# Attention beside four Strassen-style products on one NeuronCore: GpSimd ordered behind VectorE on their shared port, traced durations in the planner, a shorter hold for scores

## Chip, core and metric

One NeuronCore of one Trainium2 chip runs the whole program. The metric is device time in microseconds (us), the median over executions. Before the change it is 2990.05 us (2988.33 to 2990.17 in 3 runs).

## What is computed

Two independent blocks, joined along the last axis, all in fp32 with S = 2048, D = 1024, 32 heads of 32:

```python
qkv = x @ wqkv                                  # A: attention
p = softmax(q @ k.T * 32**-0.5); o = p @ v      # per head
a = concat(o) @ wo
re = xb @ dft_hid_re.T; im = xb @ dft_hid_im.T  # B: Fourier mixing
b = dft_seq_re @ re - dft_seq_im @ im
out = concat([a, b], axis=-1)
```

## The kernel before

**Dense work.** The four dense products (qkv, the two of block B, the output projection) are each cut into 2 by 2 blocks and done with seven products instead of eight, which needs sums and differences of blocks of both operands. Each operand tile of 128x512 is then split into a high half (a cast to the fast matmul format, L477, on VectorE or in some stages ScalarE) and a low half (tile minus high half, L480, on GpSimd or VectorE), and every product is three matmuls: high*high, low*high, high*low (L391, tiles `slot`, `h`, `l`). The sums of blocks are `fetch`'s tensor_tensors (L455, GpSimd or VectorE). PSUM results leave through VectorE (L629, L681, L896, L907).

**Attention.** For each head and each half row of scores a pair of matmuls (a "score pair", L1198) fills a PSUM tile `psS` of 128x1024. There are two such buffers. VectorE reads it once, writing the negated scores to `srow` and their minimum to `negm` (L1206, called the move below); ScalarE takes the exponentials and their sums from `srow` (L1212). The row maxima go back through DRAM into `qs`, and then the scores are computed a second time, transposed, 128x512 at a time (`psT`, L1328, two buffers), exponentiated by ScalarE (L1332, `pt` or `ptl`), and multiplied with V (L1347) in three runs per head whose results VectorE collects in `ot` (L1358, L1360). GpSimd or VectorE applies 1/sum (L1376).

**What sets the order.** Nothing is ordered by hand. While the program is recorded, a planner (`Plan`) plays it forward with a list of costs: at each moment of its own clock it starts, on each engine, the ready instruction of lowest rank, and that order is what each engine then runs, strictly in order. TensorE takes attention work (streams S, T, V: score pairs, transposed scores, V products) when it is ready and the dense "fills" otherwise. A score pair counts as ready `SLATE` us after its PSUM buffer is free by the plan, a transposed score `LATE` us after. The planner knows of one port that GpSimd and VectorE share: GpSimd instructions and those VectorE instructions marked `two=True` (casts, tensor_tensors from SBUF) are not started while `port` lies ahead of its clock (`choose`). That holds in the plan alone. On the chip an instruction waits for its data, for its buffer and for its engine's queue, and for nothing else.

Where the plan says that a GpSimd instruction comes after a cast, but the cast is late and the GpSimd instruction has its data, GpSimd goes first.

Of the kernel before, what the change touches and what calls it, by code (L numbers as in the profile page):

```python
# [10 lines left out]
AF = mybir.ActivationFunctionType  # L11
ALU = mybir.AluOpType
# [50 lines left out]
class Plan:  # L63
# [3 lines left out]

    LAT = 0.1
    LAT_PE = 0.2
    OVERLAP = {"ACT": 0.13, "DVE": 0.08, "POOL": 0.08}  # L70

    SLACK = {("SP", "POOL"): 2.0, ("SP", "DVE"): 2.0, ("SP", "PE"): 2.0, ("POOL", "DVE"): 0.7}
    KB_US = 360.0
    LANDING = 1.6
    QUEUE = 1.0

    def __init__(self):
        self.now = 0.0
        self.free = {e: 0.0 for e in ("PE", "ACT", "DVE", "POOL", "SP")}
        self.pending = {e: [] for e in ("ACT", "DVE", "POOL", "SP")}  # L80
        self.able = {e: [] for e in ("ACT", "DVE", "POOL", "SP")}
        self.dma = 0.0
        self.port = 0.0
        self.lane = [0.0] * 8
        self.seq = 0

    def op(self, engine, cost, emit, after=(), uses=(), rank=0.0, kb=0, order=None, other=None, lanes=1, two=False):

# [36 lines left out]

    def start(self, o, e=None):
        e = e or o.engine
        o.emit(e) if o.other else o.emit()
        o.begun = True
        self.free[e] = self.now + (o.cost if e == o.engine else o.other[1])  # L130
        if e == "POOL" or e == "DVE" and o.two:
            self.port = self.free[e]
        if o.kb:
            for _ in range(o.lanes):
                t = max(self.free[e], self.lane[0])
                self.dma = max(self.dma, t) + o.kb / o.lanes / self.KB_US
                o.end = self.dma + self.LANDING
                self.lane = self.lane[1:] + [o.end]
                if o.lanes > 1:
                    self.free[e] = t + o.cost  # L140
        else:
            o.end = self.free[e]
            self.free[e] -= self.OVERLAP.get(e, 0.0)
        for t in o.then:
            t.ready = max(t.ready, self.after(o, e, t))
            t.left -= 1
            if t.left == 0:
                self._release(t)
        for t in o.soon:
            t.ready = max(t.ready, self.now)  # L150
            t.left -= 1
            if t.left == 0:
                self._release(t)
        o.then = o.soon = ()
        o.emit = None
# [56 lines left out]
def kernel(  # L212
# [11 lines left out]
    nc = tc.nc  # L224
# [26 lines left out]
    def f(ap):  # L251
        return ap.bitcast(F32)
# [31 lines left out]
    rec = const.tile([P, 2 * NS], F32, name="rec")  # L284
# [50 lines left out]

    MM, PV, SWITCH, TINY = 0.2275, 0.853, 0.40, 0.17
    ES, ET = 1.235, 0.625
    MOVE = 1.25  # L340
    MAX, EVAC, CAST, BIT = 1.22, 0.685, 0.415, 0.275
    SUB = 1.31
    ISSUE = 0.46

    LATE, SLATE = 0.25, 1.2
    HB = 0
    ACAST = 0.6
    RES = 400
    SST = 13
    LEAD = 3.0  # L350
# [2 lines left out]
    NEAR = 0.2  # L353
# [3 lines left out]
    ATT = H * (128 * MM + 16 * PV + 3 * SWITCH)  # L357

    pl = Plan()
    op = pl.op  # L360
    att_on, t_on = [True], [False]
    nbank = [0]
# [54 lines left out]
    def fetch(shape, terms, store=None, keep=None):  # L417

        box = {}
        raws, seconds, tile_of, gate = where[0]  # L420
        rank = seq()
        sign, *first = terms[0]
        loaded = len(first) == 2
        if len(terms) == 1 and not loaded:
            return first[0].get, first[0].made, first[0].users
        if keep is None:
            old, users = raws.take()
        else:
# [12 lines left out]
        for sign, *term in terms[1:]:  # L441
            other = {}
            if len(term) == 2:
                gold, gusers = seconds.take()

                def load(src=term[0], other=other):
                    other["q"] = tile_of(shape, "g", len(seconds.users))
                    nc.sync.dma_start(other["q"], src)

                q = op("SP", ISSUE, load, gold + term[1] + gate, [gusers], rank, 256, seconds)  # L450
            else:
                other["k"], q, gusers = term[0], term[0].made, term[0].users

            def add(e, sign=sign, other=other, a=None if last is not None else first[0]):
                (nc.gpsimd if e == "POOL" else nc.vector).tensor_tensor(  # L455
                    out=dest(), in0=dest() if a is None else a.get(), in1=other["q"] if "q" in other else other["k"].get(), op=ALU.add if sign > 0 else ALU.subtract)

            last = op("POOL", SUB, add, old + [first[0].made if last is None else last, q], [users, gusers] + ([first[0].users] if last is None else []),
                      rank, 0, raws if keep is None and last is None else None, other=("DVE", ADD, 20 + rank), two=True)
            old = []  # L460
        if keep is not None:
            keep.made = last
        if store is not None:
            store[1].append(op("SP", ISSUE, lambda: nc.sync.dma_start(store[0], dest()), [last], [users], rank, 256))
        return dest, last, users
# [3 lines left out]
    def halves(raw, made, users, hi, lo, old, mine, order=(None, None)):  # L469

        rank = seq()

        def high(e=None):
            if e == "ACT":
                nc.scalar.activation(hi(), raw(), AF.Copy)
            else:
                nc.vector.tensor_copy(hi(), raw())  # L477

        def low(e):
            (nc.gpsimd if e == "POOL" else nc.vector).tensor_tensor(out=lo(), in0=raw(), in1=f(hi()), op=ALU.subtract)  # L480

        a = op("DVE", CAST, high, [made] + old[0], [users, mine[0]], 10 + rank, 0, order[0], ("ACT", ACAST, 25 + rank) if spare[0] else None, two=True)
        b = op("POOL", SUB, low, [a] + old[1], [users, mine[0], mine[1]], rank, 0, order[1], other=("DVE", ADD, 25 + rank), two=True)
        return a, b
# [687 lines left out]
    def scores(h):  # L1172
        ST = {}
# [11 lines left out]
        for n, (qt, c) in enumerate([(k % 4, k // 4) for k in range(8)] + [divmod(k, 2) for k in range(8, 32)]):  # L1185
            old, users = psS_r.take()
            own = h > 0 and qt < 4
            box = {}
# [29 lines left out]
            b = op("DVE", MOVE if h else MAX, mx, [a] + (sold if n == 0 else []) + (rold if h else []), [users, suse, *([ruse] if h else [])], 0)  # L1218
# [19 lines left out]
            nc.vector.tensor_reduce(out=box["l"][:, 0], in_=ST["negm"].rearrange("p c n -> p n c"), axis=AX.X, op=ALU.min)  # L1238

        def low():  # L1240
            nc.vector.tensor_tensor(out=box["l"][:, 1], in0=ST["nm"], in1=f(box["l"])[:, 0], op=ALU.subtract)

        b = op("DVE", TINY, high, maxes + lold, [luse, suse], -2)
        a = op("DVE", TINY, nmin, maxes + nold, [nuse, suse], -2)
# [14 lines left out]
    def sums(h):  # L1259
        ST, suse, nuse, exps, _ = mine[h]  # L1260
        box = {}
        told, tuse = small["tw"].take()

        def sub():
            box["t"] = sm.tile([P, 2, NS], F32, name="tt", bufs=1)
            for c in range(2):
                nc.vector.tensor_tensor(out=box["t"][:, c], in0=ST["nm"], in1=ST["negm"][:, c], op=ALU.subtract)

        def ex():
            nc.scalar.activation(box["t"], box["t"], AF.Exp)  # L1270

        def inv():
            w = box["t"]
            l = rec[:, 0:NS]
            nc.vector.tensor_tensor(out=w, in0=w, in1=ST["sums"], op=ALU.mult)
            nc.vector.tensor_reduce(out=l, in_=w.rearrange("p c n -> p n c"), axis=AX.X, op=ALU.add)
            nc.vector.reciprocal(l, l)
            box["l"] = sm.tile([P, 2 * NS], F32, name="ll", bufs=1)
            nc.vector.transpose(box["l"], rec)

        def spread():
            rt[h] = att_low().tile([P, NB], F32, name="rt", bufs=1)
            r = r_d[h][0:NS].rearrange("(j q) p -> j (q p)", j=4)
            for j in range(4):
                nc.sync.dma_start(rt[h][j * DH : j * DH + DH], r[j : j + 1].broadcast_to([DH, NB]))

        a = op("DVE", 0.24, sub, exps + told, [tuse, suse, nuse], -2, two=True)
        b = op("ACT", BIT, ex, [a], [tuse], -2)
        c = op("DVE", 0.84, inv, [b], [tuse, suse], -2, two=True)
        e = op("SP", ISSUE, lambda: nc.sync.dma_start(r_d[h].rearrange("q (g p) -> g q p", g=4), box["l"]), [c], [tuse], -2, 32)  # L1290
        rold, ruse = rt_r.take()
        g = op("SP", ISSUE, spread, [e, *rold], [ruse], -2, 256, lanes=4)
        rts[h] = (g, ruse)
# [224 lines left out]
```

## Time and profile before

| | |
|---|---|
| median of 3 runs | 2990.05 us (2988.33 to 2990.17) |
| profiled execution, device time | 2990.43 us |
| its span on the core | 2988.7 us |
| TensorE busy | 2957.1 us, 99% |
| VectorE busy | 2395.0 us, 80% |
| ScalarE busy | 2301.3 us, 77% |
| GpSimd busy | 930.1 us, 31% |
| granted TensorE clock, mean | 0.998 |

In the profile PE is TensorE's matmuls, PEld its weight loads, DVE VectorE, ACT ScalarE, POOL GpSimd, SP the queue that issues the DMAs. L and a number is a line of the kernel. A row of the timeline has the start, the duration, the engine, line and operation, the tiles, how many equal neighbours were merged, and in brackets the idle time before it with what ended it. Matmuls overlap, so that a busy TensorE can still be waiting: what counts is the distance between starts.

### The profile page before, as it was taken

To read this page: it belongs to the slowest core of one execution; us is meant where nothing else is said; L and a number is where in the kernel's file an instruction comes from. 1 tells how busy PE (TensorE), PEld (TensorE's weight loads), DVE (VectorE), ACT (ScalarE), POOL (GpSimd) and SP (SyncE) were. 2 spreads that over 40 slices of the span, in tenths; PEclk is the share of its full clock that TensorE was granted. 3 is DMA by queue.
4 is the path that set the end of the run, shared out by engine and by line. 5 is a ranking of instruction groups with operands and counts; after the bars stand their busy time and mean duration, and the time that the engine had idled before them with its cause. 6 is when DMAs were issued, how large, how long until landed. Compare 5 with 4: busy or idle time off the path is not lost.

```text
span 2988.7 us, 45652 instructions
## 1 busy us (share of the span) xinstructions
PE 2957.1 (99%) x14912; PEld 2145.3 (72%) x14912; DVE 2395.0 (80%) x4180; ACT 2301.3 (77%) x4316; POOL 930.1 (31%) x688
## 2 busy tenths in 40 slices
PE   9999999999999999999999999999999999999999
PEld 7887776677677677767776676777777767677787
DVE  7779788688877877887678888888787888887796
ACT  4336887888788888888888888888988888786321
POOL 2315345122212332222112353323212245343142
PEclk9999999999999999999999999999999999999999
DMA  9976657666626644554435675545433586466762
GB/s 338 360 233 201 200 180 249 193 219 218 209 68 200 203 148 142 180 179 145 139 110 155 197 240 170 165 152 171 129 112 99 185 267 211 149 187 200 266 207 99
DMA packets 376582, 558.59 MB, mean 187 GB/s; under 512 B 111100, under 2 KB 111100, under 8 KB 376220
## 3 DMA queue, kind: packets, MB, share of 16 engines
q1 hardware_dynamic: 376344, 555.68, 58.1%
q8 instruction: 117, 1.92, 0.3%
q14 instruction: 121, 0.99, 0.1%
HBM read 402.42 MB, written 153.11 MB: 186 GB/s over the span
## 4 chain that ended last, share of the span: by engine, by line
PE 90%; DVE 3%; ACT 3%; DMA 1%; issue 1%; SPq 0%; POOL 0%; DVEq 0%; POOLq 0%
PE pd L391 40%; PE pd L1347 15%; PE psT L1328 15%; PE psS L1198 14%; PE psT L391 7%; ACT srow L1212 2%; ACT pt L1332 1%; DVE srow L1206 1%; DVE slot L477 1%; DMA c<-u_d 0%; ACT ptl L1332 0%; DMA raw<-in_wd 0%; DVE negm L1208 0%; DVE h L477 0%; DMA rt<-r_d 0%
## 5 line engine op out<-in xcount | busy, mean ns | idle before, releaser
L1206 DVE TENSOR_SCALAR_CACHE_REDUCE srow<-psS 128x1024 f32<-128x1024 f32 x992 | 1203.1, 1220 | 211.2 <-ACT srow L1212 135.8
L1212 ACT ACTIVATE srow<-srow,negm 128x1024 f32<-128x1024 f32 x992 | 1197.1, 1214 | 15.1 <-DVE srow L1206 14.8
L1332 ACT ACTIVATE pt<-psT 128x512 f32<-128x512 f32 x1618 | 924.3, 643 | 254.9 <-PE psT L1328 238.1
L391 PE MATMUL pd<-slot,h 128*128 128x512 f32 x3352 | 1111.4, 391 | 4.8 <-DVE ot L1358 1.8
L1328 PE MATMUL psT<-qs,ks 128*128 128x512 f32 x2048 | 752.5, 396 | 5.6 <-ACT pt L1332 3.5
L391 PEld LDWEIGHTS pd<-slot,h 128*128 128x128 f32 x3352 | 630.1, 188 | 144.7 <-issue 4.2
L391 PE MATMUL pd<-slot,l 128*128 128x512 f32 x1676 | 654.4, 390 | 1.0 <-POOL l L480 1.0
L1328 PEld LDWEIGHTS psT<-qs,ks 128*128 128x128 f32 x2048 | 381.5, 188 | 157.5 <-ACT srow L1212 28.5
L480 POOL TENSOR_TENSOR l<-raw,h 128x512 fp32r<-128x512 f32 x167 | 226.1, 1355 | 796.0 <-DVE h L477 576.9
L1198 PE MATMUL psS<-ks,qs 128*128 128x512 f32 x1552 | 471.1, 391 | 1.3 <-DVE srow L1206 1.2
L1347 PE MATMUL pd<-pt,vt 128*32 128x512 f32 x3236 | 396.6, 597 | 1.6 <-DVE slot L896 1.1
L455 POOL TENSOR_TENSOR raw<-raw,g 128x512 f32<-128x512 f32 x221 | 295.7, 1344 | 317.8 <-issue 58.3
L391 PEld LDWEIGHTS pd<-slot,l 128*128 128x128 f32 x1676 | 315.2, 188 | 68.2 <-POOL l L480 1.8
L1198 PEld LDWEIGHTS psS<-ks,qs 128*128 128x128 f32 x1552 | 290.9, 188 | 63.9 <-DVE srow L1206 3.2
L1332 ACT ACTIVATE ptl<-psT 128x512 f32<-128x512 f32 x430 | 249.0, 639 | 109.7 <-PE psT L1328 102.8
L480 POOL TENSOR_TENSOR slot<-raw,slot 128x512 fp32r<-128x512 f32 x151 | 213.6, 1422 | 355.8 <-DVE slot L477 225.6
L1212 ACT ACTIVATION_READ_ACCUMULATOR srow<-srow,negm 128x1 f32 x992 | 257.7, 260 | 0.0
L1347 PEld LDWEIGHTS pd<-pt,vt 128*32 128x32 f32 x3236 | 102.3, 110 | 191.3 <-issue 182.4
L391 PE MATMUL pd<-slot,slot 128*128 128x512 f32 x768 | 189.6, 391 | 0.2 <-DVE e L681 0.2
L1360 DVE TENSOR_TENSOR ot<-ot,pd 128x512 f32<-128x512 f32 x64 | 43.9, 685 | 161.3 <-PE pd L1347 161.3
L1347 PE MATMUL pd<-ptl,vt 128*32 128x512 f32 x860 | 165.9, 600 | 4.2 <-DVE e L681 3.5
L391 PEld LDWEIGHTS pd<-slot,slot 128*128 128x128 f32 x768 | 144.2, 188 | 31.5 <-DVE e L681 0.5
(126 smaller groups left out, 2451.7 us busy)
## 6 DMA issues: line engine op xcount, KB each, us to landing
raw<-in_ct SPq DMA_DIRECT2D x224, 256.0 KB
g<-in_ct SPq DMA_DIRECT2D x128, 256.0 KB
qk_d<-e SPq DMA_DIRECT2D x52, 512.0 KB
qs<-qk_d SPq DMA_DIRECT2D x128, 192.0 KB
ks<-qk_d SPq DMA_DIRECT2D x128, 192.0 KB
raw<-ab_d SPq DMA_DIRECT2D x96, 256.0 KB
c<-u_d SPq DMA_DIRECT2D x88, 256.0 KB
g<-ab_d SPq DMA_DIRECT2D x80, 256.0 KB
```

The source lines that it names most:

```text
L391: nc.tensor.matmul(box["ps"], a[1]((a[0].hi, a[0].lo)[u]()), b[1]((b[0].hi, b[0].lo)[v]()), start=k == 0, stop=k == n - 1)
L455: (nc.gpsimd if e == "POOL" else nc.vector).tensor_tensor(out=dest(), in0=dest() if a is None else a.get(), in1=other["q"] if "q" in other ...
L477: nc.vector.tensor_copy(hi(), raw())
L480: (nc.gpsimd if e == "POOL" else nc.vector).tensor_tensor(out=lo(), in0=raw(), in1=f(hi()), op=ALU.subtract)
L1198: nc.tensor.matmul(p[:, i * NB : i * NB + NB], (QX[0] if own else QS[h % 2])[:, qt * P : qt * P + P], KS[h % 2][:, c * 1024 + i * NB : c * ...
L1206: nc.vector.tensor_scalar(box["s"], box["p"], -1.0, None, op0=ALU.mult, op1=ALU.min, accum_out=ST["negm"][:, c, qt : qt + 1])
L1212: nc.scalar.activation(box["s"], box["s"], AF.Exp, scale=-1.0, bias=ST["negm"][:, c, qt : qt + 1], accum_out=ST["sums"][:, c, qt : qt + 1])
L1328: nc.tensor.matmul(box["p"], KS[h % 2][:, t * P : t * P + P], QS[h % 2][:, j * NB : j * NB + NB], start=True, stop=True)
L1332: nc.scalar.activation(box["t"], box["p"], AF.Exp)
L1347: nc.tensor.matmul(po["p"][j * DH : j * DH + DH, :], VT[h][:, k, :], box["t"], start=(k == t0), stop=(k == t), tile_position=(0, j * DH),)
L1360: nc.vector.tensor_tensor(out=po["o"], in0=po["o"], in1=po["p"], op=ALU.add)
```

## The change

Three things, in one diff. `start` now keeps what an instruction's `emit` returns. After a VectorE instruction that uses the port it remembers that instruction; a GpSimd instruction that the plan starts after it, and within 2.5 us (`NEAR`) of its end, gets a semaphore wait on it. The costs of the planner are replaced by others. And `SLATE`, the hold of score pairs, falls from 1.2 to 0.25 us. Functions that emit more than one instruction return the last.

```diff
-    OVERLAP = {"ACT": 0.13, "DVE": 0.08, "POOL": 0.08}
+    OVERLAP = {"ACT": 0.15, "DVE": 0.08, "POOL": 0.08}
+    NEAR = 2.5
...
+        self.held = self.behind = None
...
-        o.emit(e) if o.other else o.emit()
+        made = o.emit(e) if o.other else o.emit()
         o.begun = True
         self.free[e] = self.now + (o.cost if e == o.engine else o.other[1])
         if e == "POOL" or e == "DVE" and o.two:
             self.port = self.free[e]
+        if e == "DVE" and o.two:
+            self.held = made, self.free[e]
+        elif e == "POOL" and self.held is not None and self.held[1] > self.now - self.NEAR:
+            self.behind(made, self.held[0])
...
-    MM, PV, SWITCH, TINY = 0.2275, 0.853, 0.40, 0.17
-    ES, ET = 1.235, 0.625
-    MOVE = 1.25
+    MM, PV, SWITCH, TINY = 0.2272, 0.86, 0.30, 0.17
+    ES, ET = 1.31, 0.64
+    MOVE = 1.23
...
-    LATE, SLATE = 0.25, 1.2
+    LATE, SLATE = 0.25, 0.25
     HB = 0
-    ACAST = 0.6
+    ACAST = 0.63
...
     pl = Plan()
+    pl.behind = lambda a, b: tc.add_manual_dep(a.ins, b.ins.name, mybir.DependencyInfo(mybir.DependencyClass.Sync, mybir.DependencyReason.DATA), reason="port")
```

MM is a matmul, PV and SWITCH are parts of a V product, ES and ET the two exponentials, MOVE the move, ACAST a cast on ScalarE. Since every cost enters the plan's clock, the order of all five engines is new, from the first rows on. Two places show how. In the changed program the lines are six or seven numbers higher (L455 is L462, L480 is L486, L391 is L398, L1198 is L1204, L1328 is L1335).

GpSimd's rows in the second dense product, before, with the semaphores that each waits for (DMAHW are DMA queues, `raw` and `g` loaded blocks, `raw<-raw,g` their sum):

```order
L455 TENSOR_TENSOR raw<-raw,g 128x512 [waits DMAHW6_49,Pool_49]
L455 TENSOR_TENSOR raw<-raw,g 128x512 [waits DMAHW7_49,Pool_49]
L455 TENSOR_TENSOR raw<-raw,g 128x512 [waits DMAHW1_49,DMAHW5_49,DMAHW0_49,DVE_49]
L455 TENSOR_TENSOR raw<-raw,g 128x512 [waits DMAHW2_49,Pool_49]
L480 TENSOR_TENSOR l<-raw,h 128x512 [waits DVE_49,PE_49]
L455 TENSOR_TENSOR raw<-raw,g 128x512 [waits DMAHW4_49,DMAHW3_49]
L455 TENSOR_TENSOR raw<-raw,g 128x512 [waits DMAHW5_49,DMAHW2_49,Pool_49]
```

The same part of GpSimd's queue in the changed program:

```order
L462 TENSOR_TENSOR raw<-raw,g 128x512 [waits DMAHW5_49,DMAHW7_49,DMAHW1_49,DVE_49]
L462 TENSOR_TENSOR raw<-raw,g 128x512 [waits DMAHW4_49,DMAHW0_49,DVE_49]
L462 TENSOR_TENSOR raw<-raw,g 128x512 [waits DMAHW2_49,DMAHW4_49,DMAHW0_49,DVE_49]
L462 TENSOR_TENSOR raw<-raw,g 128x512 [waits DMAHW1_49,DVE_49,Pool_49]
L486 TENSOR_TENSOR slot_18456<-raw,slot_18456 128x512 [waits DVE_49]
L486 TENSOR_TENSOR slot_18480<-raw,slot_18480 128x512 [waits DVE_49,PE_49]
```

Sums that waited for their loads alone now wait for VectorE too. In the whole program 425 of GpSimd's 675 tensor_tensors had a wait on VectorE, and 502 of 659 have one now; a low half waited for its own cast before, and may now wait for a later cast.

TensorE's rows at the first score pairs of the 19th head (`qx` is the copy of `qs` that these pairs read), before:

```order
L1198 MATMUL psS<-ks_490,qx 128x512 x2
L1328 MATMUL psT<-qs_489,ks_490 128x512 x2
L391 MATMUL pd<-slot_16929,h 128x512
L391 MATMUL pd<-slot_16929,l 128x512
L391 MATMUL pd<-slot_16929,h 128x512
L391 MATMUL pd<-slot_17189,h 128x512
L391 MATMUL pd<-slot_17189,l 128x512
L1198 MATMUL psS<-ks_490,qx 128x512 x2
```

And in the changed program:

```order
L1204 MATMUL psS<-ks_490,qx 128x512 x2
L398 MATMUL pd<-slot_17332,l 128x512
L398 MATMUL pd<-slot_17332,h 128x512
L398 MATMUL pd<-slot_17350,h 128x512
L398 MATMUL pd<-slot_17350,l 128x512
L1335 MATMUL psT<-qs_489,ks_490 128x512
L398 MATMUL pd<-slot_17350,h 128x512
L1335 MATMUL psT<-qs_489,ks_490 128x512
L398 MATMUL pd<-slot_17380,h 128x512
L1204 MATMUL psS<-ks_490,qx 128x512 x2
```

Between two pairs stand the same two transposed scores and about as many fills, but the transposed scores no longer follow the pair at once, and a fill stands between them.

More of the change, by code (lines that the diff above doesn't have):

```diff
@@ L454, in add @@
             def add(e, sign=sign, other=other, a=None if last is not None else first[0]):
-                (nc.gpsimd if e == "POOL" else nc.vector).tensor_tensor(
+                return (nc.gpsimd if e == "POOL" else nc.vector).tensor_tensor(
                     out=dest(), in0=dest() if a is None else a.get(), in1=other["q"] if "q" in other else other["k"].get(), op=ALU.add if sign > 0 else ALU.subtract)
@@ L474, in high @@
             if e == "ACT":
-                nc.scalar.activation(hi(), raw(), AF.Copy)
-            else:
-                nc.vector.tensor_copy(hi(), raw())
+                return nc.scalar.activation(hi(), raw(), AF.Copy)
+            return nc.vector.tensor_copy(hi(), raw())
         def low(e):
-            (nc.gpsimd if e == "POOL" else nc.vector).tensor_tensor(out=lo(), in0=raw(), in1=f(hi()), op=ALU.subtract)
+            return (nc.gpsimd if e == "POOL" else nc.vector).tensor_tensor(out=lo(), in0=raw(), in1=f(hi()), op=ALU.subtract)
         a = op("DVE", CAST, high, [made] + old[0], [users, mine[0]], 10 + rank, 0, order[0], ("ACT", ACAST, 25 + rank) if spare[0] else None, two=True)
@@ L1240, in low @@
         def low():
-            nc.vector.tensor_tensor(out=box["l"][:, 1], in0=ST["nm"], in1=f(box["l"])[:, 0], op=ALU.subtract)
+            return nc.vector.tensor_tensor(out=box["l"][:, 1], in0=ST["nm"], in1=f(box["l"])[:, 0], op=ALU.subtract)
         b = op("DVE", TINY, high, maxes + lold, [luse, suse], -2)
@@ L1266, in sub @@
             for c in range(2):
-                nc.vector.tensor_tensor(out=box["t"][:, c], in0=ST["nm"], in1=ST["negm"][:, c], op=ALU.subtract)
+                last = nc.vector.tensor_tensor(out=box["t"][:, c], in0=ST["nm"], in1=ST["negm"][:, c], op=ALU.subtract)
+            return last
         def ex():
@@ L1278, in inv @@
             box["l"] = sm.tile([P, 2 * NS], F32, name="ll", bufs=1)
-            nc.vector.transpose(box["l"], rec)
+            return nc.vector.transpose(box["l"], rec)
         def spread():
```

## The prediction

> **What bounds the kernel now.** I read the page first, then the waits of TensorE, then the timeline at the places where it waits.
>
> ```profile
> PE 2957.1 (99%) x14912; PEld 2145.3 (72%) x14912; DVE 2395.0 (80%) x4180; ACT 2301.3 (77%) x4316; POOL 930.1 (31%) x688
> ```
>
> TensorE is the bound, and the change leaves its 14912 matmuls as they are. So the change can only win or lose the time in which TensorE stands still. The view of waits, for TensorE alone, says how much that is:
>
> ```profile
> PE psT L391 <- ACT slot L475: 6.8, 1, 6.8
> PE psT L1328 <- ACT pt L1332: 3.5, 10, 0.6
> PE pd L1347 <- DVE e L681: 3.5, 2, 2.8
> PE psS L1198 <- DVE srow L1206: 2.9, 3, 1.7
> PE psT L1328 <- DVE e L629: 2.0, 1, 2.0
> PE pd L391 <- DVE ot L1358: 1.8, 1, 1.8
> PE pd L391 <- DVE ot L1360: 1.4, 1, 1.4
> PE pd L391 <- POOL l L480: 1.0, 2, 0.6
> ```
>
> The first row is the start of the program, which stays. The other seven hold 16.1 us, and the rows left out are of about 1 us or less each, some 4 us together: 20 us, 0.7% of the span. That is nearly all that a better order can save. Most of these waits end on VectorE, and the timeline shows why VectorE is late:
>
> ```profile
> 755.24 0.39 PE L391 MATMUL pd<-slot,l 128*128 128x512 f32 x1
> 755.47 0.39 PE L1328 MATMUL psT<-qs,ks 128*128 128x512 f32 x1
> 755.72 0.68 DVE L480 TENSOR_TENSOR slot<-raw,slot 128x512 fp32r<-128x512 f32 x1
> ...
> 755.93 1.62 POOL L480 TENSOR_TENSOR e<-e 128x512 fp32r<-128x512 f32 x1 [12.38 <-DVE e L477]
> ...
> 756.32 1.51 DVE L477 CAST slot<-raw 128x512 fp32r<-128x512 f32 x1
> ...
> 757.75 0.67 DVE L1360 TENSOR_TENSOR ot<-ot,pd 128x512 f32<-128x512 f32 x1
> ...
> 758.35 1.21 DVE L1206 TENSOR_SCALAR_CACHE_REDUCE srow<-psS 128x1024 f32<-128x1024 f32 x1
> ...
> 759.63 0.73 PE L1198 MATMUL psS<-ks,qx 128*128 128x512 f32 x2 [1.73 <-DVE srow L1206]
> ```
>
> GpSimd begins at 755.93. The cast that VectorE begins at 756.32 takes 1.51 us and ends 0.28 us after GpSimd's 757.55. Its usual length is the median here:
>
> ```profile
> L477 DVE CAST h<-raw x321: 379/421/1546, 169.8 to 2824.2; 128x512 fp32r<-128x512 f32 x161
> ```
>
> So a cast of 0.42 us loses 1.09 us behind GpSimd, the move behind it (758.35) comes late, and TensorE stands 1.73 us for a score buffer. The two matmuls at 755.24 and 755.47 begin 0.23 us apart but last 0.39, and idle time is counted from the 0.39: a wait costs 0.16 us more than its row says.
>
> **The wait of GpSimd.** The program numbers its instructions in the order in which the plan starts them. By that order this cast stood ahead of the GpSimd row that blocked it. I went through all casts and tensor_tensors of VectorE that are stretched beside a GpSimd row in the attention stage: in 59, from the one at 260.85 to one in the pair at 2699.83 below, GpSimd ran ahead of the plan (54 us of VectorE's time), and in 75 it stood ahead in the plan too (25 us). The new wait orders the 59 and does nothing for the 75. Four more of TensorE's long waits follow such rows:
>
> ```profile
> 260.85 1.52 DVE L477 CAST slot<-raw 128x512 fp32r<-128x512 f32 x1
> ...
> 264.16 0.73 PE L1328 MATMUL psT<-qs,ks 128*128 128x512 f32 x2 [1.99 <-DVE e L629]
> ...
> 449.52 1.76 DVE L480 TENSOR_TENSOR l<-raw,h 128x512 fp32r<-128x512 f32 x1
> ...
> 451.93 0.50 PE L391 MATMUL pd<-slot,h 128*128 128x512 f32 x1 [1.79 <-DVE ot L1358]
> ...
> 783.33 1.78 DVE L480 TENSOR_TENSOR e<-e 128x512 fp32r<-128x512 f32 x1
> ...
> 786.90 0.72 PE L1198 MATMUL psS<-ks,qs 128*128 128x512 f32 x2 [1.00 <-DVE srow L1206]
> ...
> 2609.96 1.78 DVE L480 TENSOR_TENSOR slot<-raw,slot 128x512 fp32r<-128x512 f32 x1
> ...
> 2612.99 0.51 PE L391 MATMUL pd<-slot,h 128*128 128x512 f32 x1 [1.41 <-DVE ot L1360]
> ...
> 2699.83 2.38 DVE L480 TENSOR_TENSOR slot<-raw,slot 128x512 fp32r<-128x512 f32 x2
> ...
> 2700.06 1.61 POOL L480 TENSOR_TENSOR l<-raw,h 128x512 fp32r<-128x512 f32 x1 [1.79 <-DVE h L477]
> ```
>
> The five waits are 1.73 + 1.99 + 1.79 + 1.00 + 1.41 = 7.9 us, with 0.16 us each 8.7 us. I take all five as gone: **-8.7**. Of the smaller waits some follow a stretched row within 9 us as well; for these I take **-3** (0 to -5).
>
> Two of the five also cost clock. In the next rows the second column is TensorE's busy time with its matmuls in brackets, and the third from the end the granted clock:
>
> ```profile
> 264.80:268.20 3.40, 3.40 (x10) 2.50 (x9) 2.19 (x6) 3.40 (x6) 0.09 (x1) 0.50 0.97 298
> 452.50:455.90 3.40, 3.40 (x10) 2.61 (x9) 2.26 (x5) 2.53 (x5) 0.00 (x0) 0.50 0.75 252
> 503.70:510.50 6.80, 5.88 (x28) 1.36 (x32) 3.46 (x6) 0.00 (x0) 0.56 (x1) 0.50 0.94 248
> ```
>
> Behind the waits of 1.99 and 1.79 us the clock is halved for 3.4 us: 10 matmuls where 15 would fit at 0.23 us, so 1.1 us each, **-2.2**. (The third stretch, behind the 2.8 us wait for `e` of the second view, has no such row ahead of it; I leave it.) The Trainium skill, "TensorE: Matmul & The Clock Gate", Part 1, says that the clock falls after at least one idle window of about 3.4 us. By that rule waits of 2 us would cost no clock, and the sum would end 2.2 us higher; the granted clock of 0.50 in these rows speaks against it, and 2983 us would lie in my range anyway.
>
> What the wait costs: GpSimd stands until a cast (0.42 us) or a tensor_tensor (0.68 us) is done, and what is queued behind it, the low halves, comes later by as much. The Trainium skill, "SBUF — State Buffer", Who interferes with whom, says that issue order decides who blocks, for the whole instruction. By that rule the change removes no blocking, it moves it to GpSimd. The rows at 755.93 agree: GpSimd met VectorE's L480 and took 1.62 us.
>
> ```profile
> L480 POOL TENSOR_TENSOR l<-raw,h x167: 1280/1300/1803, 245.5 to 2716.0; 128x512 fp32r<-128x512 f32 x167
> ```
>
> The median of such a row is 1.30 us, so GpSimd lost 0.32 where VectorE lost 1.09: which of the two goes first decides the price. GpSimd is 31% busy, and TensorE waits for it 1.0 us in 2 waits, so the cover is wide. If it goes, 77 more waits (502 for 425) of at most 0.68 us would be 52 us of GpSimd's time; at TensorE's 2 waits of 0.5 us I take **+1** (0 to +8, a wait of TensorE in every fifth of them).
>
> **The shorter hold.** A score pair needs the move of the pair before the last, which frees its buffer. The next rows are three times such a move's end (the accumulator row) and the pair that needs it:
>
> ```profile
> 354.25 0.08 DVE L1206 DVE_READ_ACCUMULATOR srow<-psS 128x1 f32 x1
> ...
> 354.88 0.39 PE L1198 MATMUL psS<-ks,qs 128*128 128x512 f32 x1
> ...
> 1589.58 0.08 DVE L1206 DVE_READ_ACCUMULATOR srow<-psS 128x1 f32 x1
> ...
> 1591.09 0.39 PE L1198 MATMUL psS<-ks,qs 128*128 128x512 f32 x1
> ...
> 2662.96 0.07 DVE L1206 DVE_READ_ACCUMULATOR srow<-psS 128x1 f32 x1
> ...
> 2664.03 0.39 PE L1198 MATMUL psS<-ks,qs 128*128 128x512 f32 x1
> ```
>
> At 1589.66 the buffer is free and the pair comes 1.43 us later. This is the usual case: 651 of 990 pairs lie between 1.2 and 1.75 us, the hold of 1.2 with the planner's latency. With 0.95 us less, the usual pair keeps some 0.5 us, and what today lies under 1.0 us would be a wait. Those are 66 pairs, from 354.88 (0.55 us) to 2664.03 (1.00 us), at 27 places; what they lack of 1.0 us is 30 us added up, and 16 us if at each place only the worst counts, since one wait of TensorE serves all that follow. 2.9 us of it is waited for already. 48 of the 66 pairs come within 9 us of a row of the 59. Take these away, and 18 pairs with 8 us are left: **+6** (0 to +27). The price is zero at the low end if the new order has no late moves. What the shorter hold itself could win I cannot find in the profile: while a pair is held TensorE has other work.
>
> **The new costs.** They lie nearer to the trace. A score exponential, for one, runs from 1500.71 to 1502.04:
>
> ```profile
> 1500.71 1.24 ACT L1212 ACTIVATE srow<-srow,negm 128x1024 f32<-128x1024 f32 x1
> ...
> 1501.75 0.29 ACT L1212 ACTIVATION_READ_ACCUMULATOR srow<-srow,negm 128x1 f32 x1
> ```
>
> That is 1.33 us, where the plan had 1.235 and has 1.31. Transposed scores should wait less for ScalarE (3.5 us in 10 waits, 5.1 with 0.16 each), also because a fill now stands between them: **-2** (0 to -5). All else that the new order moves, loads and stores above all, I cost at nothing, since TensorE's waits on DMA do not show among its rows; the cover is the fills, and if it goes the waits are of the size of the 2.8 us one.
>
> **Sum.** -8.7 - 3 - 2.2 + 1 + 6 - 2 = -8.9 us. The profiled execution took 2990.4, so 2981.5; it lies 0.4 above the median of 2990.05, so **2981 us**.
>
> **Rivals.** (1) *Slower: the hold was the cover.* If VectorE is late for other reasons than GpSimd's early rows (the 75 stay, and GpSimd that waits for a late VectorE is itself late for the next cast), nothing of the first terms is won and all 27 places fall short: +16 - 2.9 = +13, 3003 us; with each pair counted, 3017. It decides from about 30 waits of 0.5 us on score buffers, the 15 us that the other terms win. For it: one score wait in today's trace already costs 1.73 us. Against it: 48 of the 66. (2) *The waits do nothing.* 425 of 675 GpSimd rows waited on VectorE already and collided all the same; if the new ones are met before they count, VectorE stays as late as now, the hold costs a few us and the new costs win 2: 2990 us. (3) *All of it goes.* The 20 us of waits with 0.16 each and all three clock stretches, 25 us, and nothing new: 2966 us.
>
> **Chances.** My forecast 0.52, with a range of its own of 2972 to 2989; rival 1 0.20; rival 2 0.18; rival 3 0.10. The range that should hold 8 times in 10 reaches from 2966 to 3004: it takes in rival 3 and the lower price of rival 1. A measurement here can tell about 0.2%, 6 us: faster is under 2984, slower over 2996. Of the forecast 0.42 is faster and 0.10 the same; rival 3 is faster; rival 2 is the same but for 0.03; rival 1 is slower but for 0.02. Faster 0.52, same 0.27, slower 0.21.
>
> **What would show it.** Casts (L477) over 1 us get rare between 250 and 2700 us, and VectorE's busy time falls by some 50 us: the wait works. TensorE's rows on `ot`, `e` and `srow` of over 1 us go, and the two half-clock stretches with them. Score waits rise in number but stay under 0.5 us each: the hold is paid as I said. If TensorE's waits on `srow` add up to more than 15 us, rival 1 is right; if stretched casts are as many as now, rival 2. A wait on a new cause, a DMA or GpSimd's low halves, over 5 us in all would make the sum wrong in a place where I put nothing.

## The result and the profile after

The changed kernel takes **2958.45 us** (2957.39 to 2959.65 in 4 runs) where the kernel before takes 2990.11 beside it (2988.33 to 2990.84): a ratio of **0.9896 [0.9883, 0.9908]**, 31.7 us less. The forecast was 2981 with a range of 2966 to 3004, so the time lies 7.5 us below the range. The profiled execution took 2957.99 us, its span is 2956.1 us, and the mean granted clock rose from 0.998 to 1.000.

The busy times of the changed kernel, from its page, and the shares of its chain by engine, from the same page:

```profile
PE 2940.3 (99%) x14912; PEld 2145.2 (73%) x14912; DVE 2345.2 (79%) x4198; ACT 2300.3 (78%) x4314; POOL 860.8 (29%) x672
...
PE 98%; DVE 1%; ACT 1%; DMA 0%; POOL 0%; issue 0%; SPq 0%; DVEq 0%; POOLq 0%
```

VectorE is busy for 49.8 us less and GpSimd for 69.3 us less, at nearly the same work: 16 tensor_tensors have moved from GpSimd (675 before, 659 now) to VectorE, which is 21 us of GpSimd's gain at 1.30 us each. The chain is TensorE's to 98%, where it was 90%. The view of TensorE's waits in the changed kernel, complete:

```profile
PE psT L398 <- ACT slot L482: 7.2, 1, 7.2
PE psT L1335 <- ACT pt L1339: 1.5, 2, 1.0
PE psS L1204 <- DVE srow L1212: 1.0, 3, 0.6
PE pd L398 <- POOL l L486: 0.7, 2, 0.5
PE pd L398 <- DVE h L483: 0.5, 2, 0.4
PE psT L1335 <- ACT ptl L1339: 0.2, 1, 0.2
PE pd L398 <- DVE l L486: 0.2, 1, 0.2
```

Without the program's start (the first row) 4.1 us are left of about 20; no wait on `ot` or `e` is listed any more, and none is longer than 1.0 us. GpSimd's own gain is seen in the durations of its tensor_tensors, minimum, median and maximum in ns. One form of the kernel before (the other, `l<-raw,h`, stands in the prediction), then both of the changed kernel:

```profile
L480 POOL TENSOR_TENSOR slot<-raw,slot x151: 1274/1322/2872, 152.9 to 2936.7; 128x512 fp32r<-128x512 f32 x151
```

```profile
L486 POOL TENSOR_TENSOR slot<-raw,slot x154: 1279/1297/1314, 152.6 to 2908.3; 128x512 fp32r<-128x512 f32 x154
L486 POOL TENSOR_TENSOR l<-raw,h x152: 1280/1298/1312, 217.6 to 2698.2; 128x512 fp32r<-128x512 f32 x152
```

Up to 1803 and 2872 ns before, 1314 at most now. Of all 659 tensor_tensors of GpSimd one alone takes over 1319 ns, a sum (L462) of 1746: a GpSimd instruction that starts behind VectorE's last one on the port is hardly ever held up.

**A finer count of TensorE's waits.** The view of waits starts counting at a matmul's modelled end. In what follows "by starts" means: the distance between the starts of two neighbouring matmuls beyond the usual 0.227 us (0.522 after a V product, 0.318 ahead of one; distances inside a V product are left out), added up where it is over 0.15 us. The half-clock time is that of all stretches with a granted clock of about 0.5, the program's last 3 us left out. "Score waits" are those ahead of a score pair, "T waits" those ahead of a transposed score, by what ended them. "Fills left" is how many matmuls of the dense stages other than the last projection still stood behind the last V product.

| kernel | waits by starts, us (count) | half clock, us | score waits on `srow` | T waits on ScalarE | fills left |
|---|---|---|---|---|---|
| before | 36.3 (81) | 13.7 | 4.3 (7) | 9.3 | 172 |
| after | 9.7 (27) | 0 | 2.1 (5) | 2.9 | 115 |

The waits by starts fall by 26.6 us; a matmul's longer distance at half clock is counted among them. Outside this count stand V products at half clock, 2.9 us before and none now, and distances that are longer by less than 0.15 us, 3.7 us more before. Together that is 33.2 us, and the profiled span is 32.6 us shorter. So the whole gain is TensorE standing still less or running at half clock less, and the question is which of the three parts of the change did it.

### The profile page after: what moved, and what is told of

Same layout as the page of the kernel before. It is cut to its first block, busy times and chain, and to the rows that moved or that the text cites. A ratio compares the mean times of both kernels' runs of the same rounds, so it can differ in the third digit from the quotient of the medians.

```text
span 2956.1 us, 45723 instructions
## 1 busy us (share of the span) xinstructions
PE 2940.3 (99%) x14912; PEld 2145.2 (73%) x14912; DVE 2345.2 (79%) x4198; ACT 2300.3 (78%) x4314; POOL 860.8 (29%) x672
## 4 chain that ended last, share of the span: by engine, by line
PE 98%; DVE 1%; ACT 1%; DMA 0%; POOL 0%; issue 0%; SPq 0%; DVEq 0%; POOLq 0%
PE pd L398 44%; PE psT L1335 16%; PE psS L1204 16%; PE pd L1354 15%; PE psT L398 7%; DVE srow L1212 1%; ACT srow L1218 0%; ACT pt L1339 0%; DMA er<-in_xa 0%; DMA g<-in_ct 0%; DVE h L483 0%; POOL slot L486 0%; POOL l L486 0%; ACT ptl L1339 0%; DVE l L486 0%
## 5 line engine op out<-in xcount | busy, mean ns | idle before, releaser
L398 PE MATMUL pd<-slot,h 128*128 128x512 f32 x3384 | 1169.9, 390 | 0.5 <-DVE h L483 0.5
L1335 PE MATMUL psT<-qs,ks 128*128 128x512 f32 x2048 | 793.7, 394 | 1.7 <-ACT pt L1339 1.5
L398 PEld LDWEIGHTS pd<-slot,h 128*128 128x128 f32 x3384 | 635.2, 188 | 136.5 <-issue 1.7
L398 PE MATMUL pd<-slot,l 128*128 128x512 f32 x1692 | 659.6, 390 | 0.9 <-POOL l L486 0.7
L1335 PEld LDWEIGHTS psT<-qs,ks 128*128 128x128 f32 x2048 | 381.5, 188 | 139.4 <-issue 42.8
L1204 PE MATMUL psS<-ks,qs 128*128 128x512 f32 x1552 | 470.4, 391 | 1.0 <-DVE srow L1212 0.8
L486 POOL TENSOR_TENSOR l<-raw,h 128x512 fp32r<-128x512 f32 x152 | 197.2, 1297 | 758.9 <-DVE h L483 349.6
L462 POOL TENSOR_TENSOR raw<-raw,g 128x512 f32<-128x512 f32 x211 | 273.0, 1300 | 376.5 <-DVE raw L462 96.2
L398 PEld LDWEIGHTS pd<-slot,l 128*128 128x128 f32 x1692 | 317.6, 188 | 69.2 <-POOL l L486 1.6
L1204 PEld LDWEIGHTS psS<-ks,qs 128*128 128x128 f32 x1552 | 290.5, 188 | 64.8 <-DVE srow L1212 3.0
L486 POOL TENSOR_TENSOR slot<-raw,slot 128x512 fp32r<-128x512 f32 x154 | 199.0, 1298 | 380.9 <-DVE l L486 97.6
L398 PE MATMUL pd<-slot,slot 128*128 128x512 f32 x768 | 194.7, 390 | 0.0
L483 DVE CAST h<-raw 128x512 fp32r<-128x512 f32 x321 | 146.6, 458 | 25.9 <-PE pd L398 19.2
L398 PEld LDWEIGHTS pd<-slot,slot 128*128 128x128 f32 x768 | 144.2, 188 | 31.0
```

The lines of the kernel that those rows point to most:

```text
L398: nc.tensor.matmul(box["ps"], a[1]((a[0].hi, a[0].lo)[u]()), b[1]((b[0].hi, b[0].lo)[v]()), start=k == 0, stop=k == n - 1)
L462: return (nc.gpsimd if e == "POOL" else nc.vector).tensor_tensor(out=dest(), in0=dest() if a is None else a.get(), in1=other["q"] if "q" i ...
L483: return nc.vector.tensor_copy(hi(), raw())
L486: return (nc.gpsimd if e == "POOL" else nc.vector).tensor_tensor(out=lo(), in0=raw(), in1=f(hi()), op=ALU.subtract)
L1204: nc.tensor.matmul(p[:, i * NB : i * NB + NB], (QX[0] if own else QS[h % 2])[:, qt * P : qt * P + P], KS[h % 2][:, c * 1024 + i * NB : c * ...
L1335: nc.tensor.matmul(box["p"], KS[h % 2][:, t * P : t * P + P], QS[h % 2][:, j * NB : j * NB + NB], start=True, stop=True)
```

## The experiments

The main theory: GpSimd's early rows carry the loss, so the wait alone brings most of the gain. Against it stand two rivals: that the hold and the costs, which I had priced at +6 and -2, bring it; and that any new order is a few us better or worse, whatever it is meant to do. Each diff is against the changed kernel unless it says otherwise; every kernel ran beside the kernel before on the same chip, which took 2987.9 to 2990.1 us, so a difference between kernels of two chips is uncertain by about 2 us.

**wait_only**: the waits, with the old costs and the old hold. Its order on every engine is that of the kernel before.

```diff
-    OVERLAP = {"ACT": 0.15, "DVE": 0.08, "POOL": 0.08}
+    OVERLAP = {"ACT": 0.13, "DVE": 0.08, "POOL": 0.08}
...
-    MM, PV, SWITCH, TINY = 0.2272, 0.86, 0.30, 0.17
-    ES, ET = 1.31, 0.64
-    MOVE = 1.23
+    MM, PV, SWITCH, TINY = 0.2275, 0.853, 0.40, 0.17
+    ES, ET = 1.235, 0.625
+    MOVE = 1.25
...
-    LATE, SLATE = 0.25, 0.25
+    LATE, SLATE = 0.25, 1.2
...
-    ACAST = 0.63
+    ACAST = 0.6
```

> The kernel before with GpSimd's new waits alone: its old costs, its hold of 1.2 us, so the order of every engine is that of before. Port theory (the gain is that GpSimd no longer runs ahead of VectorE): the 58 early rows of the attention stage go, with them the waits of TensorE behind them and two of three half-clock stretches, 15 to 17 us: about 2974 us. Cost theory (the gain is a plan that keeps step with the chip): within 4 us of 2990. Hold theory: 2990.

Measured 2973.3 us (2971.42 to 2975.26), ratio 0.9952 [0.9937, 0.9967]: 15.3 us less than the kernel before on that chip (2988.64). Since the order is the same, the place of the first timeline of the prediction can be found again by counting matmuls; here it is:

```profile
745.73 0.42 DVE L483 CAST slot<-raw 128x512 fp32r<-128x512 f32 x1
...
746.07 0.68 DVE L1367 TENSOR_TENSOR ot<-ot,pd 128x512 f32<-128x512 f32 x1
...
746.29 1.29 POOL L486 TENSOR_TENSOR e<-e 128x512 fp32r<-128x512 f32 x1 [13.15 <-DVE slot L483]
...
746.66 1.22 DVE L1212 TENSOR_SCALAR_CACHE_REDUCE srow<-psS 128x1024 f32<-128x1024 f32 x1
...
747.09 0.39 PE L1335 MATMUL psT<-qs,ks 128*128 128x512 f32 x1
...
747.95 0.72 PE L1204 MATMUL psS<-ks,qx 128*128 128x512 f32 x2 [0.46 <-DVE srow L1212]
```

GpSimd now waits for the cast ("<-DVE slot L483") and starts 0.14 us after its end. The cast takes 0.42 us where it took 1.51, GpSimd 1.29 where it took 1.62, and the score pair follows the matmul ahead of it by 0.86 us instead of 2.12 (from 757.51 to 759.63). At all five places of the prediction the same two matmuls are compared:

| matmul (start before, us) | distance to the one ahead before | in wait_only |
|---|---|---|
| 264.16 | 2.39 | 1.47 |
| 451.93 | 2.18 | 0.23 |
| 759.63 | 2.12 | 0.86 |
| 786.90 | 1.38 | 0.23 |
| 2612.99 | 1.80 | 0.23 |

Three of the five waits go wholly and two in part, 6.9 us in all, where I had taken 8.7. The one ahead of the third half-clock stretch, which I had left in, went as well: 3.20 us became 0.81. In return two waits grew, by starts from 0.5 to 2.4 us and from 0.9 to 2.0, and behind each the clock is halved for 3.4 us. This kernel's view of waits has them as the longest of two rows:

```profile
PE pd L398 <- DVE h L483: 2.6, 2, 1.7
...
PE pd L398 <- DVE e L687: 2.2, 1, 2.2
```

**no_wait** and **costs_only**: the new costs without the waits, with the short hold and with the old one. The first has the changed kernel's order. In both

```diff
-        elif e == "POOL" and self.held is not None and self.held[1] > self.now - self.NEAR:
+        elif False:
```

and in costs_only also

```diff
-    LATE, SLATE = 0.25, 0.25
+    LATE, SLATE = 0.25, 1.2
```

> The changed kernel without GpSimd's new waits, all else as changed, so the order of every engine is that of after. Port theory: the early rows come back, and with a hold of 0.25 us score pairs wait for what VectorE loses: over 2980, up to 3000 us. Cost theory: the order of after is in step by itself: under 2965 us.

> The kernel before with the new costs alone: no new waits, hold of 1.2 us. Cost theory: most of the 32 us, so 2960 to 2970 us. Port theory: only what TensorE waits for ScalarE, 2 to 5 us: 2985 to 2990 us, with about as many early rows (58 in the attention stage) as before.

Measured 2983.56 us (2979.97 to 2986.49), 0.9985 [0.9975, 0.9994], for no_wait; 3004.34 (3002.98 to 3005.79), 1.0056 [1.0041, 1.0071], for costs_only. Neither theory had costs_only above 3000 us. The waits are worth 25.1 us in the changed kernel's order, more than in the old one, and without them the rest of the change wins next to nothing. What they take away there is this, from the waits of no_wait:

```profile
PE psS L1204 <- DVE srow L1212: 9.9, 21, 1.4
```

The changed kernel has 1.0 us in 3 waits in its place.

**no_costs**, **hold_only** and **no_hold** complete the table: waits and short hold with the old costs; the short hold alone; waits and new costs with the old hold. no_costs has the four cost edits of wait_only, hold_only has them and the `elif False`, and no_hold is

```diff
-    LATE, SLATE = 0.25, 0.25
+    LATE, SLATE = 0.25, 1.2
```

> The changed kernel with the old costs: new waits and hold of 0.25 us. Port theory: within 8 us of 2958, the waits on ScalarE coming back. Cost theory: about 2985 or slower, since plan and chip drift apart and no hold covers it.

> The kernel before with the hold of 0.25 us alone: no new waits, old costs. Port theory: the 48 score pairs that come behind early GpSimd rows, and the rest of the 66, now make TensorE wait: slower than before by 5 to 25 us, 2995 to 3015 us. Hold theory (the shorter hold is a gain by itself): under 2985 us.

> The changed kernel with the hold of 1.2 us: new waits, new costs. If the hold costs time where it is paid (my term of the prediction, +6), this is at or under 2958 us, near 2952. If the shorter hold is what wins the 15 us that the waits alone did not, it is near 2973 us. If the new costs with the long hold make a bad order whatever the waits do, it is over 2980 us.

| us (ratio with its interval) | old costs, hold 1.2 | old costs, hold 0.25 | new costs, hold 1.2 | new costs, hold 0.25 |
|---|---|---|---|---|
| without the waits | the kernel before | 3005.03 (1.0057 [1.004, 1.0073]) | 3004.34 (1.0056 [1.0041, 1.0071]) | 2983.56 (0.9985 [0.9975, 0.9994]) |
| with the waits | 2973.3 (0.9952 [0.9937, 0.9967]) | 2975.84 (0.9959 [0.9945, 0.9973]) | 2987.61 (1.0 [0.9991, 1.0009]) | 2958.45 (0.9896 [0.9883, 0.9908]) |

Down each column the waits win: 15.3, 29.2, 16.7 and 25.1 us, with the kernel before taken at 2988.6. The two kernels of a column have the same order on every engine. Along the rows nothing is a sum. The short hold alone costs 16.4 us; with the waits it costs 2.5, which is less than two orders differ by chance (luck_mm and luck_old, below); with waits and new costs it wins 29.2. The new costs alone cost 15.7 us; with the waits and the short hold they win 17.4. The counts by starts say why:

| kernel | waits by starts, us (count) | half clock, us | score waits on `srow` | T waits on ScalarE | fills left |
|---|---|---|---|---|---|
| wait_only | 22.5 (55) | 10.2 | 0.8 (2) | 6.2 | 172 |
| hold_only | 47.4 (107) | 17.1 | 15.8 (31) | 13.4 | 163 |
| no_costs | 26.5 (65) | 10.2 | 3.9 (6) | 13.0 | 163 |
| no_wait | 29.4 (66) | 6.8 | 15.2 (28) | 1.8 | 115 |
| costs_only | 54.6 (89) | 27.3 | 5.5 (7) | 4.6 | 0 |
| no_hold | 37.8 (55) | 17.1 | 1.9 (2) | 5.4 | 0 |

*Short hold without the waits*: the score pairs wait for the moves that early GpSimd rows make late, 31 and 28 waits with 15 us; with the waits 6 and 5 are left.

*Short hold with the old costs*: the transposed scores wait for ScalarE, 13.0 us. In no_costs the rows of TensorE and ScalarE at 2528 us, with the clock behind them:

```profile
2528.63 0.50 PE L1335 MATMUL psT<-qs,ks 128*128 128x512 f32 x1 [0.77 <-ACT pt L1339]
2528.90 1.21 ACT L1218 ACTIVATE srow<-srow,negm 128x1024 f32<-128x1024 f32 x1
...
2530.03 1.13 ACT L1339 ACTIVATE ptl<-psT 128x512 f32<-128x512 f32 x2
2530.73 1.28 PE L1335 MATMUL psT<-qs,ks 128*128 128x512 f32 x2 [0.90 <-ACT ptl L1339]
2530.99 1.22 ACT L1218 ACTIVATE srow<-srow,negm 128x1024 f32<-128x1024 f32 x1
...
2533.07 1.23 ACT L1218 ACTIVATE srow<-srow,negm 128x1024 f32<-128x1024 f32 x1
```

```profile
2530.90:2537.70 6.80, 6.61 (x14) 4.36 (x15) 4.31 (x10) 4.60 (x10) 0.00 (x0) 0.50 0.59 187
```

ScalarE works without a gap: one score exponential and two transposed ones take 2.09 us (2528.90 to 2530.99, and 2.08 to 2533.07). The plan lets the next instruction start `OVERLAP` before the end, so with the old costs it counts (1.235 - 0.13) + 2 x (0.625 - 0.13) = 2.095 us, within 0.01 us of what the chip takes, and a transposed score has nothing to spare. With the new costs it counts 1.16 + 2 x 0.49 = 2.14. TensorE's waits there cost 6.8 us of half clock on top.

*New costs with the old hold*: no fills are left when attention ends. In no_hold TensorE has done 5750 fills by the 1000th score pair, where the kernel before has done 5559 and the changed one 5629. The waits of no_hold (the first row holds the program's start too), its timeline and its chain at the end of attention, and the clock there:

```profile
PE psT L398 <- ACT slot L482: 17.4, 3, 9.7
...
PE psT L398 <- DVE slot L486: 2.4, 1, 2.4
```

```profile
2821.39 4.71 PE L398 MATMUL psT<-slot,slot 128*128 128x512 f32 x12 [9.71 <-ACT slot L482]
...
2848.89 1.65 PE L398 MATMUL psT<-slot,slot 128*128 128x512 f32 x3 [2.41 <-DVE slot L486]
```

```profile
2806.39 5.41 PE pd L1354 x48
2811.82 0.70 DVE ot L1367
2812.54 0.70 DVE ot L1383
...
2814.61 4.64 DMA raw<-in_wo
2819.33 0.63 ACT slot L482
```

```profile
2814.40:2824.60 10.20, 3.21 (x7) 2.29 (x8) 5.94 (x9) 5.62 (x9) 0.00 (x0) 0.50 0.95 327
2848.60:2852.00 3.40, 3.11 (x7) 2.49 (x8) 2.65 (x5) 1.25 (x3) 0.62 (x1) 0.50 1.05 387
```

Behind the last V product come the last `ot`, its store, the loads of `wo` that stand behind the store in SP's queue (4.64 us in the chain) and the high halves, one after the other, and TensorE has nothing in the meantime: it stands 9.7 us at once. From 2800 to 2900 us the waits are 16.3 us by starts, the longer distances of 13.6 us of half clock among them: more than half of the 29.2 us between no_hold and the changed kernel. The other waits of no_hold are 21.5 us, about wait_only's 22.5, so that with the old hold the new costs won nothing elsewhere. With 115 fills left, 26 us of TensorE's time, the changed kernel has work in that place, and it has no wait by starts between 2800 and 2900 us.

**luck_mm**: how much does an order differ from one that should be as good? One cost changes by 0.1%.

```diff
-    MM, PV, SWITCH, TINY = 0.2272, 0.86, 0.30, 0.17
+    MM, PV, SWITCH, TINY = 0.2274, 0.86, 0.30, 0.17
```

> The changed kernel with one cost moved by a thousandth (a matmul 0.2274 us instead of 0.2272), which reorders the attention stage without a meaning of its own. If the gain lies in the waits, the costs and the hold, it stays within 5 us of 2958. If a good part of it is the luck of one order, it lands 8 us or more away, as the costs alone did.

Measured 2962.69 us (2960.31 to 2964.05), 0.9917 [0.9902, 0.9932]: 4.2 us more than the changed kernel.

**hold_06**: a hold half way.

```diff
-    LATE, SLATE = 0.25, 0.25
+    LATE, SLATE = 0.25, 0.6
```

> The changed kernel with a hold of 0.6 us. If the hold acts smoothly and shorter is better, between 2958 and the kernel with 1.2 us; if orders differ by luck, anywhere within 10 us of them; if my term was right and holding is cover, under 2958 us.

Measured 2970.16 us (2966.65 to 2971.85), 0.9941 [0.9926, 0.9956], with 67 fills left; 3.8 us of its waits lie between 2800 and 2900 us, and 13.7 us run at half clock. The time falls with the hold, 2987.6, 2970.2, 2958.5, while 0, 67 and 115 fills are left.

**act_costs**: of the new costs only ES, ET and ScalarE's overlap, with waits and short hold.

```diff
-    MM, PV, SWITCH, TINY = 0.2272, 0.86, 0.30, 0.17
+    MM, PV, SWITCH, TINY = 0.2275, 0.853, 0.40, 0.17
...
-    MOVE = 1.23
+    MOVE = 1.25
...
-    ACAST = 0.63
+    ACAST = 0.6
```

> New waits, hold of 0.25 us, and of the new costs ScalarE's exponentials alone (1.31, 0.64 and the overlap of 0.15); TensorE's, the move's and the cast's costs are the old ones. In the kernel with all costs old TensorE waited 13 us for ScalarE's exponentials in front of transposed scores, in the changed one 3. If ScalarE's costs are what wins the 17 us between these two, this is under 2965 us with at most 4 us of such waits; if TensorE's costs (a V product, a switch) are, it stays near 2976 us.

Measured 2963.44 us (2961.39 to 2965.44), 0.9913 [0.9899, 0.9928]: 12.4 of the 17.4 us between no_costs and the changed kernel. The waits of act_costs, of which the ScalarE rows in no_costs were 3.4 us in 7 and 2.6 in 5:

```profile
PE psS L1204 <- DVE srow L1212: 4.9, 8, 1.4
...
PE psT L1335 <- ACT pt L1339: 0.7, 2, 0.4
```

By starts the transposed scores wait 1.9 us for ScalarE instead of 13.0. So ScalarE's costs are what matters in the costs; the other 5.0 us are about luck_mm's 4.2 and are not read.

**luck_old** and **luck_old_wait**: the kernel before with one cost changed, without and with the waits. Against it the first is

```diff
-    MM, PV, SWITCH, TINY = 0.2275, 0.853, 0.40, 0.17
+    MM, PV, SWITCH, TINY = 0.2277, 0.853, 0.40, 0.17
```

and the second has the waits as well, in the first one's order.

> The kernel before with a matmul's cost of 0.2277 instead of 0.2275 us: another order without a meaning of its own, no new waits. Its distance from 2989 us is the luck of an order with the old costs: within 8 us if the changed kernel's 4 us under the same test is typical.

> The same reordered kernel with GpSimd's new waits and nothing else: the order of every engine is that of the kernel without them. Port theory: 15 us or more faster than it (15 to 29 in the four pairs so far), with no early rows left. If the waits only helped the orders tried so far, within 5 us of it.

Measured 2982.12 us (2978.69 to 2987.54), 0.9978 [0.9969, 0.9988], and 2966.55 (2964.5 to 2967.27), 0.9923 [0.9908, 0.9937]. A change of 0.1% in one cost wins 6.5 us by itself, and the waits win 15.6 us in this order too. luck_old_wait has 6.5 us of T waits on ScalarE, as many as wait_only, but no half-clock stretch, where wait_only has 10.2 us.

**hold_01**: a still shorter hold.

```diff
-    LATE, SLATE = 0.25, 0.25
+    LATE, SLATE = 0.25, 0.1
```

> The changed kernel with a hold of 0.1 us. With 1.2, 0.6 and 0.25 us the times are 2988, 2970 and 2958 us. If what the hold does is to slow attention, so that the fills run out before the last head, there is nothing left to win below 0.25, where 115 fills remain: 2955 to 2963 us. If a hold is a cost everywhere, under 2955 us. If the cover is now too thin (a pair keeps some 0.3 us), over 2963 us, from waits on moves.

Measured 2963.99 us (2962.61 to 2965.6), 0.9915 [0.9901, 0.993], with 105 fills left and 2.7 us of score waits in 7: 5.5 us more than the changed kernel, about what luck does. None of the twelve beats the changed kernel.

## Why the prediction was wrong

**The waits: right, in mechanism and nearly in size.** The terms -8.7, -3, -2.2 and +1 make -12.9; the waits alone win 15.3 at the same order. The sum agrees better than its parts. By starts TensorE's waits fall by 13.7 us: 6.9 at the five places, 2.4 at the wait that I had left in, and 4.5 net at all others, which is 12.2 us of shorter waits and 7.7 of longer ones.

Of the 58 stretched VectorE rows in the attention stage that my count over all runs finds behind an early GpSimd row in the kernel before (the prediction's 59), none is left in wait_only and one in the changed kernel. I had put 54 us of VectorE's time on them, and they went. But VectorE now meets GpSimd more often where the plan put GpSimd first: 146 stretched rows with 40.6 us in the changed kernel, after 75 with 25.4. That VectorE is busy 49.8 us less, nearly the forecast 50, is therefore in part luck: the dense work ahead of attention and behind it, which I had not counted, gave another 22 us, and the 16 tensor_tensors taken over from GpSimd cost 11.

The +1 for a later GpSimd was not paid where I had looked: GpSimd's time fell, and TensorE waits for it 0.7 us in 2 waits after 1.0 in 2. Rival 2 falls. I had worked out from the Trainium skill, "SBUF — State Buffer", Who interferes with whom (the engine that issues second is blocked for the whole instruction), that the change would only move the block to GpSimd. The rows agree with the rule and not with what I made of it: in the changed kernel all GpSimd tensor_tensors but one take 1319 ns or less, so GpSimd waits on the semaphore, with 29% of its time in use, and is hardly ever blocked on the port.

**The clock: half right.** The stretches behind the waits of 264.16 and 451.93 us went, as forecast, and so did the third. But wait_only has three others, so that its time at half clock falls from 13.7 to 10.2 us, 1.7 us won where I had 2.2. The changed kernel has none.

**The failed step: the new costs, -2 (0 to -5).** By the prediction's own order of terms the runs give -15.3 for the waits, +2.5 for the hold (forecast +6, 0 to +27) and **-17.4 for the costs**. The mechanism named there, transposed scores that wait less for ScalarE, is what act_costs shows. But it was sized by the "3.5 us in 10 waits" of the view of the kernel before, and it is 9.3 us by starts there and 13.0 once the hold is short; the half clock that such waits bring, 6.8 us behind the waits of 2528 us in no_costs, was not counted. One error was to price the costs and the hold each for itself, against the trace before: the shorter hold packs scores closer, and that makes the true exponential costs matter. The -17.4 holds for this pair of orders: the three other kernels with the waits, a short hold and ScalarE's new costs are 12 to 13 us faster than no_costs, and no_costs is one order alone.

**"What the shorter hold itself could win I cannot find in the profile: while a pair is held TensorE has other work."** That is the other half of the same error. Held, TensorE does fills; and these were counted as free. With the new costs attention takes more fills per pair, and with the old hold they are used up before it ends (no_hold, 0 left, 9.7 us in one wait). The supply of 172 at the end of the kernel before was never looked at.

**The ceiling: "nearly all that a better order can save", 20 us, and rival 3 at 2966.** The waits by starts are 36.3 us in 81 waits. The view, with 29 waits, misses the rest: it leaves out 52 waits, 11 us, in which the distance is longer by less than 0.31 us, and takes 0.16 us off every other wait. With the 2.9 us of V products at half clock 39 us was to be had, and 31.7 came. That is why the range ended above the result.

**Rival 1** was right about its mechanism and wrong about the condition: hold_only and no_wait have just the 15 us of score waits that were to decide it. The new waits remove them: 2.1 us are left.

**What stays open.** Orders that differ by 0.1% in one cost are 4.2 and 6.5 us apart. The three kernels with the waits, a short hold and ScalarE's new costs beside the changed one lie at 2962.7, 2963.4 and 2964.0; those with the waits and the old costs at 2966.6, 2973.3 and 2975.8. So about 5 of the 31.7 us may be this order's luck. What the hold and the costs win together on top of the waits is 14.9 us in the pair wait_only and changed kernel, but 2.6 to 3.9 us from luck_old_wait to those three: that it is more than chance is not shown, and neither is the share of each. What is shown is that the waits win in all five orders, and that new costs with the long hold, or the short hold with the old costs, bring the waits described above. How new costs without a short hold bring TensorE to take more fills per pair was seen in the count of fills and not traced through the planner.

## What to carry to other kernels

A plan that keeps two engines off a shared port holds on the chip only if something on the chip enforces it; a semaphore wait on VectorE ahead of such GpSimd instructions was worth 15 to 29 us of 2990 here in each of the five orders tried. Edits to a plan's costs and its slack are not to be priced one by one against the trace before, since each changes what the other's slack is for; and work that fills gaps is a stock, so count how much of it is left at the end of the stage. Measure waits from start to start before you say how much there is to win.

## What was not expected of the hardware

The clock does not need one long wait to fall. The half-clock stretches last 3.41 us or two or three times that, and they lie whole multiples of 3.413 us apart (264.8, 452.5 and 503.7 us before: 55.0 and 15.0 of it). I laid a grid of this step over the profiles of all fourteen kernels and counted in each cell how long TensorE had a matmul (0.227 us each, the usual distance of two starts, or until the next start). All 21 cells between 200 and 2750 us that were followed by a half clock had 0.14 to 0.402 of matmuls. Of all other cells at full clock only two were below that (0.389 and 0.391), and the next lie at 0.404 and 0.411. In no_costs waits of 0.77 and 0.90 us sit in one cell (0.375), in which five matmuls start where fifteen would fit, and halve the clock for 6.8 us; before, the wait of 1.73 us at 759.63 sits in a cell of 0.447, and the clock stays. The Trainium skill, "TensorE: Matmul & The Clock Gate", Part 1, has the free-running window of 3.4 us, and these runs agree with it; but it asks for an idle window, where here one with less than about 0.40 of matmuls was enough.

Putting the two engines in order on their port saves time on both. no_wait has the changed kernel's order without the waits: there VectorE is busy 2398.3 us and GpSimd 909.8, against 2345.2 and 860.8. GpSimd's 211 sums take 1344 ns on average in no_wait and 1300 in the changed kernel, and VectorE's casts are shorter too. From no_wait first, then from the changed kernel:

```profile
L462 POOL TENSOR_TENSOR raw<-raw,g 128x512 f32<-128x512 f32 x211 | 282.2, 1344 | 337.3 <-DMA raw<-in_ct 74.2 <-DVE raw L462 72.2 <-issue 34.0
...
L483 DVE CAST slot<-raw 128x512 fp32r<-128x512 f32 x228 | 123.0, 554 | 3.0 <-PE pd L398 1.2 <-DMA raw<-ab_d 0.7 <-DMA raw<-in_wd 0.7
```

```profile
L462 POOL TENSOR_TENSOR raw<-raw,g 128x512 f32<-128x512 f32 x211 | 273.0, 1300 | 376.5 <-DVE raw L462 96.2 <-DMA raw<-in_ct 70.9 <-issue 26.8
...
L483 DVE CAST slot<-raw 128x512 fp32r<-128x512 f32 x228 | 103.9, 470 | 7.2 <-DMA raw<-ab_d 2.3 <-PE pd L398 1.0 <-DMA raw<-in_wv 1.0
```

What remains of stretched casts and tensor_tensors is VectorE that meets a GpSimd instruction which the plan itself put first: 146 rows with 40.6 us in the attention stage of the changed kernel, where 75 with 25.4 us stood before. The waits do nothing against those.
